# MoE 2, rounds 1 to 5: the seven products of a round in the order X, Y, X, Z, X, Z, X

## The chip, the cores and the metric

The kernel runs on one core of one Trainium2 chip. The metric is the device time of one execution in microseconds. Engines: PE is TensorE (matmuls; PEld its weight loads), DVE is VectorE, ACT is ScalarE, POOL is GpSimd, SP issues most of the DMAs.

## The reference

Attention with a local mask (heads 0 to 3) or a strided one (heads 4 to 7) on 4 x 8 heads of 576 x 64; its output, as 2304 tokens x 512, goes through two feed-forward blocks:

```
h = x @ w_in                      # MoE 1: 512 -> 2048
g = h * tanh(softplus(h))         # mish
x = g @ w_out                     # 2048 -> 512
g = x @ w_gate; silu = g * sigmoid(g)   # MoE 2: 512 -> 1536
val = x @ w_val
out = (silu * val) @ w_out        # 1536 -> 512
```

All in float32. Each fp32 operand is held as two parts (a high part rounded to fp32r, and the remainder), and each product of two operands is three matmuls: high x high, high x low, low x high (`mm3`, L160).

## The kernel before

The change is in MoE 2, in `c_round`. MoE 2 goes over 12 rounds: P = r // 6 picks a pair of token chunks of 512 (0 and 1, then 2 and 3), i = r % 6 picks 256 of the 1536 hidden columns. In a round, four outputs are wanted for gate (`g`) and for val (`v`): two chunks times two halves of 128 hidden columns. They are not made by eight products of blocks but by seven, with sums of weights (S12, S34) and sums of tokens (T1 to T4), in Winograd's manner. The table PROD names them, in the order n = 0 to 6: bank, weights, half, tokens.

Each product adds into one of three PSUM banks, X, Y or Z, with one such bank for gate and one for val: n = 0, 2, 4, 6 add into X, n = 1, 3 into Z, n = 5 is alone in Y. After every product the bank's state is read: after n = 0, 1, 2 ACT copies it to SBUF (L1327), after n = 3, 4, 5 DVE adds it to one of those copies (L1332), after n = 6 ACT takes silu of gate's bank (L1342) and DVE multiplies by val's (L1278). A product that adds into a bank on must therefore wait until the bank's earlier state has been read. A product is 6 matmuls (2 x mm3) for gate and 6 for val.

Rounds 0 and 6 to 11 take the products in the order n = 0 to 6 (X Z X Z X Y X). Rounds 1 to 5 take 0, 5, 1, 2, 3, 4, 6, that is X Y Z X Z X X. After the products of round r come 4 tiles `o` of the output product of the round before (`d_tile`, L1393: DVE adds each to `acc`), in rounds 0 to 5 the small last chunk (`c4_round`, tiles `c`), and 4 to 6 more tiles `o`.

In rounds 0 to 4 the other engines also make the weights of the round to come out of raw 64-bit data: units of 4 DVE instructions (L393, L396, L401, L404) and a Square on ACT (L398), or 2 DVE instructions for a sum (L370/L376 for S12, L372/L378 for S34); then ACT casts the high part (L150) and DVE subtracts it (L155) for the low part, in the middle of the next unit. The order of gate's units, then val's, is W0, W1, S12, S34, so the last of val's weights of a round are made in that round's first products.

The order on each engine is set when the program is built. The code is written in the order of PE's work, and `fill` puts background units between, by a model of time: `clk[...]` per engine, `on_dve`/`on_act` with costs in us, `pe_at` that holds PE's clock for an operand, `free`/`lru` for the banks, `gates` from which a unit may begin. `pe_at` changes no wait of the program; waits come from the data. SP and POOL run their queues in the order of the code.

Of the kernel before, what the change touches and what calls it, by code (L numbers as in the profile page):

```python
# [12 lines left out]
ALU = mybir.AluOpType  # L13
# [42 lines left out]
NP = FF2 // 256  # L56
LATE_OUT = ((), (1,), (3,), (5,), (7,), (8, 9))
SPLIT, SPLIT2, SUM2, SQUARE, MISH, COPY, LEAD = 0.69, 0.42, 0.42, 0.67, 0.6, 0.6, 0.2
# [47 lines left out]
def local_strided_attention__mish_moe__swiglu_kernel(  # L106
# [9 lines left out]
    nc = tc.nc  # L116
# [21 lines left out]
    def pe_at(t, what=None):  # L138
        clk["pe"] = max(clk["pe"], t)
# [75 lines left out]
    plan = []  # L215
# [28 lines left out]
    for r in range(NP):  # L244
        plan.append(("gate", ("n", r, -1)))
        todo = w2_out(*LATE_OUT[r])
        for kind in "gv"[r == 0:] if r + 1 < NP else "":
            todo += w2_in(kind, r + 1, "W0", "W1", "S12", "S34")
        for key in todo:
            if key[0][2] in ("S12", "S34"):  # L250
                plan.append(("gate", ("n", r, 2 if key[0][2] == "S12" else 4)))
            wlist.append(key)
            plan.append(("unit",))
    for n, k in enumerate(("T1", "T2", "B22", "T3", "B21", "T4")):
# [482 lines left out]
    def on_dve(cost, ready, do):  # L737
        clk["dve"] = max(clk["dve"], ready) + cost
        do()
        return clk["dve"]  # L740

    def on_act(cost, ready, do):
        clk["act"] = max(clk["act"], ready) + cost
        do()
        return clk["act"]
# [305 lines left out]

    def in_round(q, P, behind_=None):
        c0, c1 = 2 * P, 2 * P + 1
        bank, keep = [{}, {}], [{}, {}]
        for n, (x, a, half, b) in enumerate(PROD):
            if b[0] == "T":
                need(("x", P, b))
            for k in range(2):
                key = ("s", q, k, a)
                need(key if key[3][0] == "S" else ("i", q * QF + 2 * k + (a == "W1")))  # L1060
                first = x not in bank[k]
                if first:
                    bank[k][x] = lru("c" + x)
                p, at = bank[k][x]
                w = wt[key]
                for j in range(2):
                    sl = slice(half * 256 + j * 128, half * 256 + j * 128 + 128)
                    xo = x_op(P, b, j)
                    mm3(p, w[:, 0, sl], w[:, 1, sl], *xo, first and j == 0, j == 1, True)
                pe = clk["pe"]  # L1070
                if n < 3:
                    tag, nb = ("u", 4) if n < 2 else ("wtmp", 2)
                    keep[k][n] = t = sb.tile([128, 512], F32, tag=tag, name="k%d" % n, bufs=nb)
                    on_act(COPY, pe, lambda: nc.scalar.copy(t, p))
                    fill()
                elif n < 6:
                    fill()
                    t = keep[k][{3: 2, 4: 1, 5: 0}[n]]
                    r = on_dve(0.69, pe, lambda: nc.vector.tensor_tensor(out=t, in0=p, in1=t, op=ALU.add))
                    if n != 4:  # L1080
                        free(at, r)
                    r = mish(t, t, r)
                    g_make(q * NCH + (c0 if n == 5 else c1), [2 * k + (n == 4)], t, r)
                else:
                    if k == 0:
                        n6["t"] = sb.tile([128, 2, 512], F32, tag="acc4", name="n6")
                    n6[k] = n6["t"][:, k], mish(n6["t"][:, k], p, pe)
                    free(at, n6[k][1])
                    fill()
            if behind_:  # L1090
                behind_(n)
        gates["in", q, P] = clk["pe"]
# [166 lines left out]
    def ld(r, *what, kinds="gv"):  # L1259
        if r >= 2 * NP:  # L1260
            return
        P, i = divmod(r, NP)
        for x in what:
            for kind in "p" if x in (0, 1) else kinds:
                t = w2_slot(kind, r, x)
                if P == 0 and (2 * i + x in sum(LATE_OUT, ()) if kind == "p" else i > (kind == "g")):
                    continue
                half = x == "W1" and P == 1
                sl = slice(256 * half, 512)
                nc.sync.dma_start(t[:, :, sl].bitcast(F32), wd[kind, i, x][:, :, sl])  # L1270
                whole[kind, i, x] = moved("sp", clk["pe"], 0.5 if half else 1)
# [15 lines left out]
    def finish(r, f, c):  # L1287
# [9 lines left out]
        else:  # L1297
            for f in range(2):
                fs[r, f, c] = h[:, :, f * 256:f * 256 + 256], ready

    def c_round(r, between):
        P, i = divmod(r, NP)
        bank = {k: {} for k in "gv"}
        keep = {k: {} for k in "gv"}
        for n in (0, 5, 1, 2, 3, 4, 6) if 0 < r < NP else range(7):
            x, a, half, b = PROD[n]
            while (P, b) not in op_at:
                assert head()
                run_head()
            o = ops[P][b]  # L1310
            for k in "gv":
                need((k, i, a))
                first = x not in bank[k]
                if first:
                    bank[k][x] = lru("c" + x + k)
                p, at = bank[k][x]
                pe_at(op_at[P, b], (P, b))
                w = w2_slot(k, r, a)
                for j in range(2):
                    sl = slice(half * 256 + j * 128, half * 256 + j * 128 + 128)  # L1320
                    mm3(p, w[:, 0, sl], w[:, 1, sl], o[:, j, 0], o[:, j, 1], first and j == 0, j == 1, True)
                pe = clk["pe"]
                if n < 3:
                    tag, nb = ("u", 4) if n < 2 else ("wtmp", 2)
                    t = sb.tile([128, 512], F32, tag=tag, name="k%d" % n, bufs=nb)
                    keep[k][n] = t
                    on_act(COPY, pe, lambda: nc.scalar.copy(t, p))  # L1327
                    fill()
                elif n < 6:
                    fill()  # L1330
                    t = keep[k][{3: 2, 4: 1, 5: 0}[n]]
                    ready = on_dve(SPLIT, pe, lambda: nc.vector.tensor_tensor(out=t, in0=p, in1=t, op=ALU.add))  # L1332
                    if n != 4:
                        free(at, ready)
                    if k == "g":
                        s, silu = t, on_act(MISH, ready, lambda: nc.scalar.activation(out=t, in_=t, func=AF.Silu))  # L1336
                    else:
                        f, c = {3: (0, 1), 4: (1, 1), 5: (0, 0)}[n]
                        product(r, f, c, s, t, max(silu, ready))
                elif k == "g":  # L1340
                    s = sb.tile([128, 512], F32, tag="px", name="s21", bufs=2)
                    silu = on_act(MISH, pe, lambda: nc.scalar.activation(out=s, in_=p, func=AF.Silu))  # L1342
                    free(at, silu)
                    fill()
                else:
                    fill()
                    product(r, 1, 0, s, p, max(silu, pe), at)
            gates["n", r, n] = clk["pe"]
            between(n)
            fill()  # L1350

    def c4_round(r):
# [66 lines left out]
    with tc.manual_schedule():  # L1419
# [81 lines left out]
        for r in range(2 * NP + 1):  # L1501
            P = r // NP
            if r < 2 * NP:
                gates["n", r, -1] = clk["pe"]
                if r:
                    ld(r + 1, "W0")

                def between(n):
                    if r == 0:
                        if n == 5:  # L1510
                            settle("tiles")
                            ld(0, 0, 1)
                            ld(1, "W0", "S12", "S34")
                        return
                    if n == 2:
                        ld(r + 1, "S12")
                    if n == 4:
                        ld(r + 1, "S34")

                c_round(r, between)  # L1520
            if r > 0:
                for t in range(4):
                    d_tile(r - 1, 1, t)
            if r < 2 * NP:
                finish(r, 0, 0)
                finish(r, 1, 0)
                if P == 0:
                    c4_round(r)
                ld(r + 1, "W1")
            if r > 0:  # L1530
                for t in range(4):
                    d_tile(r - 1, 0, t)
                if r <= NP:
                    for t in range(2):
                        d_tile(r - 1, 4, t)
            if 0 < r < 2 * NP - 1:
                ld(r, 0, 1)
            if r == 2 * NP - 2:
                ld(r + 1, 0, 1)
# [86 lines left out]
```

## Time and profile before

| | |
|---|---|
| median of 3 runs | 865.35 us (865.15 to 868.08) |
| profiled execution | 864.76 us, span 863.0 us |
| PE busy | 851.2 us, 99% of the span |
| DVE busy | 624.3 us, 72% |
| ACT busy | 446.2 us, 52% |
| POOL busy | 175.1 us, 20% |
| MoE 2, rounds 1 to 5 | 467.16 to 665.82 us |

The profiled execution's own time is 1.76 us over its span. In the timeline a row is a group of like instructions; the duration of a group of matmuls reaches to the modelled end of its last, so that it overlaps the next by about 0.16 us. From start to start six matmuls of 128x512 take 1.36 us.

### The profile page before, as it was taken

The numbers are of one execution on the slowest core, as the hardware profiler recorded it, in microseconds if no ns is written. First come the engines' busy times: TensorE is split into PE (matmuls) and PEld (weight loads), VectorE is DVE, ScalarE is ACT, GpSimd is POOL, SyncE is SP. The second block draws the span as 40 slices with busy tenths as digits, with TensorE's granted clock in tenths as the row PEclk, the third lists the DMA queues.
The fourth block names the chain that finished last, engine by engine and source line by source line (L and its number), as shares of the span: only waits on it lengthen the run. The fifth ranks groups of instructions, "written<-read, shape, count | busy, mean of one in ns | idle before, by whom it ended". The sixth has DMA issues, their size and how long they took to land.

```text
span 863.0 us, 14267 instructions
## 1 busy us (share of the span) xinstructions
PE 851.2 (99%) x5216; PEld 707.2 (82%) x5216; DVE 624.3 (72%) x1348; ACT 446.2 (52%) x1063; POOL 175.1 (20%) x195
## 2 busy tenths in 40 slices
PE   8999999999999999999999999999999999999998
PEld 5788778888888888888888888887878888888886
DVE  6998879597668658685779999999987434432534
ACT  7999956565756565644645544444354322332230
POOL 5652311002010010002113202030216112211211
PEclk9999999999999999999999999999999999999999
DMA  9875344617867594753547655646491574464322
GB/s 300 267 222 165 114 162 189 223 51 150 276 153 226 139 267 109 220 216 123 226 164 231 221 211 191 225 170 239 147 320 60 181 270 139 153 209 136 108 84 98
DMA packets 46006, 158.72 MB, mean 184 GB/s; under 512 B 4976, under 2 KB 8688, under 8 KB 43632
## 3 DMA queue, kind: packets, MB, share of 16 engines
q1 hardware_dynamic: 40320, 129.81, 43.9%
q0 software_dynamic: 4464, 20.45, 9.5%
q10 hardware_dynamic: 1152, 7.55, 2.6%
q8 instruction: 41, 0.67, 0.3%
q14 instruction: 29, 0.24, 0.1%
HBM read 101.17 MB, written 56.62 MB: 183 GB/s over the span
## 4 chain that ended last, share of the span: by engine, by line
PE 91%; DVE 6%; issue 2%; ACT 1%; POOL 0%; DVEq 0%; POOLq 0%
PE y L160 23%; PE o L160 17%; PE h L160 8%; PE cX L160 8%; PE cXv L160 6%; PE cXg L160 6%; PE cZ L160 4%; PE c L160 3%; PE cZv L160 3%; PE cZg L160 3%; PE cY L160 2%; PE cYv L160 2%; PE cYg L160 2%; PE xp L599 2%; PE tp L562 2%
## 5 line engine op out<-in xcount | busy, mean ns | idle before, releaser
L160 PE MATMUL y<-g,w 128*128 128x512 f32 (+1 forms) x960 | 202.3, 370 | 0.0
L160 PEld LDWEIGHTS y<-g,w 128*128 128x128 f32 x960 | 166.7, 189 | 29.6
L160 PE MATMUL o<-wr,fs 128*128 128x512 f32 x648 | 149.6, 390 | 0.0
L160 PEld LDWEIGHTS o<-wr,fs 128*128 128x128 f32 x648 | 121.4, 188 | 25.0
L155 POOL TENSOR_TENSOR fs<-k,fs 128x512 fp32r<-128x512 f32 x36 | 50.2, 1393 | 269.3 <-ACT fs L150 251.5
L1393 DVE TENSOR_TENSOR acc<-acc,o 128x512 f32<-128x512 f32 x90 | 61.5, 684 | 35.5 <-PE o L160 35.2
L150 ACT CAST fs<-k 128x512 fp32r<-128x512 f32 x36 | 22.4, 622 | 80.6 <-DVE k L1278 35.5
L160 PE MATMUL h<-xh,w 128*128 128x512 f32 (+1 forms) x208 | 61.5, 361 | 0.0
L516 ACT ACTIVATE pt<-pt,sm 128x64 f32<-128x64 f32 (+1 forms) x160 | 55.9, 363 | 3.7 <-DVE sm L502 3.7
L160 PE MATMUL cXg<-T,wr 128*128 128x512 f32 x216 | 55.5, 393 | 2.2 <-DVE k L1332 2.0
L160 PE MATMUL cXv<-T,wr 128*128 128x512 f32 x216 | 55.2, 391 | 1.9 <-DVE k L1332 1.9
L1141 POOL DMA_DIRECT2D yd<-yv x20 | 16.0, 802 | 187.4 <-ACT yv L1135 187.4
L1327 ACT COPY k<-cXg 128x512 f32<-128x512 f32 x24 | 14.1, 587 | 75.8 <-PE cXg L160 75.8
L160 PEld LDWEIGHTS cXg<-T,wr 128*128 128x128 f32 x216 | 40.2, 188 | 12.4 <-DVE k L1332 4.3
L160 PEld LDWEIGHTS cXv<-T,wr 128*128 128x128 f32 x216 | 40.3, 188 | 11.5 <-DVE k L1332 3.2
L1332 DVE TENSOR_TENSOR k<-cZg,k 128x512 f32<-128x512 f32 x12 | 8.3, 688 | 49.5 <-PE cZg L160 49.5
L160 PEld LDWEIGHTS h<-xh,w 128*128 128x128 f32 x208 | 37.0, 189 | 5.2 <-issue 0.2
L1135 ACT COPY yv<-y 128x512 f32<-128x512 f32 x40 | 23.2, 588 | 28.7 <-PE y L160 26.2
L545 POOL TENSOR_TENSOR pt<-pt,sm 128x192 f32<-128x192 f32 (+2 forms) x48 | 34.1, 729 | 16.2 <-DVE sm L538 12.7
L160 PE MATMUL h<-xl,w 128*128 128x512 f32 (+1 forms) x104 | 36.4, 350 | 0.0
L1336 ACT ACTIVATE k<-k 128x512 f32<-128x512 f32 x36 | 22.8, 632 | 25.5 <-DVE k L1332 25.4
L160 PE MATMUL c<-yh,wr 128*128 128x256 f32 x192 | 35.5, 283 | 0.0
(180 smaller groups left out, 1807.8 us busy)
## 6 DMA issues: line engine op xcount, KB each, us to landing
raw<-in_w_dram SPq DMA_DIRECT2D x44, 512.0 KB, 4.9
rawl<-in_w_dram SPq DMA_DIRECT2D x24, 512.0 KB, 4.3
yd<-yv POOLq DMA_DIRECT2D x20, 512.0 KB, 5.9
wr<-wd_p SPq DMA_DIRECT2D x18, 512.0 KB, 4.4
wr<-wd_g_S SPq DMA_DIRECT2D x16, 512.0 KB, 3.4
wr<-wd_v_S SPq DMA_DIRECT2D x14, 512.0 KB, 4.6
wr<-wd_g_W SPq DMA_DIRECT2D x10, 512.0 KB, 6.3
wd_v_W<-wr SPq DMA_DIRECT2D x10, 512.0 KB, 5.0
```

The source lines that it names most:

```text
L150: nc.scalar.copy(hi, src)
L155: eng.tensor_tensor(out=lo, in0=src, in1=hi.bitcast(F32), op=ALU.subtract)
L160: nc.tensor.matmul(o, lhsT=lhs, rhs=rhs, start=first and i == 0, stop=last and i == 2, skip_group_check=more)
L516: nc.scalar.activation(out=pt[:, x], in_=pt[:, x], func=AF.Exp, scale=-1.0, bias=sm[:, 0, x:x + 1], accum_out=sm[:, 1, x:x + 1],)
L545: nc.gpsimd.tensor_tensor(out=a, in0=a, in1=sm[:, 1, x].unsqueeze(2).to_broadcast(a.shape), op=ALU.mult)
L562: nc.tensor.transpose(tp[:, 128 * x:128 * x + 128], a, ident)
L599: nc.tensor.matmul(banks[r][64 * h:64 * h + 64, o:o + nq - skip], lhsT=v_t[s][rows, i, 64 * h:64 * h + 64], rhs=ts[rows, c0 + skip:c0 + nq ...
L1135: t = on_act(COPY if nt == 512 else 0.4, clk["pe"], lambda: nc.scalar.copy(dst, p[:, :nt]))
L1141: nc.gpsimd.dma_start(yd[c][:, e0:e + 1], src, **kw)
L1327: on_act(COPY, pe, lambda: nc.scalar.copy(t, p))
L1336: s, silu = t, on_act(MISH, ready, lambda: nc.scalar.activation(out=t, in_=t, func=AF.Silu))
L1393: ready = on_dve(SPLIT, clk["pe"], lambda: nc.vector.tensor_tensor(out=x, in0=x, in1=o, op=ALU.add))
```

## The change

The order of the products in rounds 1 to 5 becomes 0, 5, 2, 1, 4, 3, 6 (X Y X Z X Z X): n = 2 is moved ahead of n = 1, and n = 4 ahead of n = 3. `LAST` says after which product the weights S12 and S34 are used for the last time, so that their gates and reloads stay at the same places (after the fourth and the sixth product). And `read` keeps the modelled time at which a bank was read, in `in_round` (MoE 1) and in `c_round`, and `pe_at` holds the next product on that bank to it.

```diff
@@ in_round (MoE 1)
-        bank, keep = [{}, {}], [{}, {}]
+        bank, keep, read = [{}, {}], [{}, {}], {}
...
+                pe_at(read.get((k, x), 0.0), (n, x))
...
-                    on_act(COPY, pe, lambda: nc.scalar.copy(t, p))
+                    read[k, x] = on_act(COPY, pe, lambda: nc.scalar.copy(t, p))
...
-                    r = on_dve(0.69, pe, lambda: nc.vector.tensor_tensor(out=t, in0=p, in1=t, op=ALU.add))
+                    read[k, x] = r = on_dve(0.69, pe, lambda: nc.vector.tensor_tensor(out=t, in0=p, in1=t, op=ALU.add))
@@ c_round (MoE 2)
+    ROUND = range(7), (0, 5, 2, 1, 4, 3, 6)
+    LAST = {False: {2: "S12", 4: "S34"}, True: {1: "S12", 3: "S34"}}
...
-        for n in (0, 5, 1, 2, 3, 4, 6) if 0 < r < NP else range(7):
+        read = {}
+        for n in ROUND[0 < r < NP]:
...
-                pe_at(op_at[P, b], (P, b))
+                pe_at(max(op_at[P, b], read.get((k, x), 0.0)), (P, b, k))
...
-                    on_act(COPY, pe, lambda: nc.scalar.copy(t, p))
+                    read[k, x] = on_act(COPY, pe, lambda: nc.scalar.copy(t, p))
...
-                    ready = on_dve(SPLIT, pe, lambda: nc.vector.tensor_tensor(out=t, in0=p, in1=t, op=ALU.add))
+                    read[k, x] = ready = on_dve(SPLIT, pe, lambda: nc.vector.tensor_tensor(out=t, in0=p, in1=t, op=ALU.add))
...
             gates["n", r, n] = clk["pe"]
-            between(n)
+            done = LAST[0 < r < NP].get(n, n)
+            gates["n", r, done] = clk["pe"]
+            between(done)
@@ the gates of the units and the reloads on SP
-                plan.append(("gate", ("n", r, 2 if key[0][2] == "S12" else 4)))
+                plan.append(("gate", ("n", r, key[0][2])))
...
-                    if n == 2:
-                        ld(r + 1, "S12")
-                    if n == 4:
-                        ld(r + 1, "S34")
+                    if n in ("S12", "S34"):
+                        ld(r + 1, n)
```

What this moves on PE, in each of the rounds 1 to 5 (round 1 here; `cXg` is gate's bank X, `cZv` val's bank Z; T and B are the token operands; `+` is the order after the change):

```order
 L160 MATMUL cYg<-B_5126,wr 128x512 x6
 L160 MATMUL cYv<-B_5126,wr 128x512 x6
+L160 MATMUL cXg<-T_5046,wr 128x512 x6
+L160 MATMUL cXv<-T_5046,wr 128x512 x6
 L160 MATMUL cZg<-T_4800,wr 128x512 x6
 L160 MATMUL cZv<-T_4800,wr 128x512 x6
-L160 MATMUL cXg<-T_5046,wr 128x512 x6
-L160 MATMUL cXv<-T_5046,wr 128x512 x6
+L160 MATMUL cXg<-T_5022,wr 128x512 x6
+L160 MATMUL cXv<-T_5022,wr 128x512 x6
 L160 MATMUL cZg<-B_5109,wr 128x512 x6
 L160 MATMUL cZv<-B_5109,wr 128x512 x6
```

The pair on T_5046 (n = 2) stands ahead of the pair on T_4800 (n = 1), and the pair on T_5022 (n = 4) ahead of that on B_5109 (n = 3); the last pair on X (n = 6) follows in both orders. The rest of PE's order is the same.

On DVE, the stretch of round 2 that reads the fifth and the sixth product (k are the SBUF copies, rawl and wt a unit of weights). Before:

```order
L155 TENSOR_TENSOR wr<-wt_5804,wr 128x512
L1332 TENSOR_TENSOR k_5846<-cZg,k_5846 128x512
L1332 TENSOR_TENSOR k_5860<-cZv,k_5860 128x512
L1278 TENSOR_TENSOR k_5846<-k_5846,k_5860 128x512
L393 TENSOR_SCALAR wt_5877<-rawl 128x512
L1332 TENSOR_TENSOR k_5826<-cXg,k_5826 128x512
L396 SCALAR_TENSOR_TENSOR wt_5877<-rawl,wt_5877 128x512
L1332 TENSOR_TENSOR k_5835<-cXv,k_5835 128x512
L1278 TENSOR_TENSOR k_5826<-k_5826,k_5835 128x512
```

And after the change:

```order
L155 TENSOR_TENSOR wr<-wt_5804,wr 128x512
L1337 TENSOR_TENSOR k_5845<-cXg,k_5845 128x512
L1337 TENSOR_TENSOR k_5860<-cXv,k_5860 128x512
L1279 TENSOR_TENSOR k_5845<-k_5845,k_5860 128x512
L393 TENSOR_SCALAR wt_5877<-rawl 128x512
L1337 TENSOR_TENSOR k_5825<-cZg,k_5825 128x512
L396 SCALAR_TENSOR_TENSOR wt_5877<-rawl,wt_5877 128x512
L1337 TENSOR_TENSOR k_5833<-cZv,k_5833 128x512
L1279 TENSOR_TENSOR k_5825<-k_5825,k_5833 128x512
```

The reads of X and of Z have changed places; no background instruction stands elsewhere between them. On ACT the copies of X and of Z (the third and the fourth product) change places in the same way, in round 2 without any other row moving. The orders of SP and POOL are the same, and so is everything in MoE 1.

## Rows read from the trace of the kernel before

**Rows 1.** The page, busy time of each engine over the span.

```profile
PE 851.2 (99%) x5216; PEld 707.2 (82%) x5216; DVE 624.3 (72%) x1348; ACT 446.2 (52%) x1063; POOL 175.1 (20%) x195
```

**Rows 2.** Waits of PE, whole span: line, releaser, us in total, times, longest.

```profile
PE cXg L160 <- DVE k L1332: 2.0, 2, 1.4
PE cXv L160 <- DVE k L1332: 1.9, 3, 0.6
```

**Rows 3.** Timeline of PE, round 2: start, duration, instructions, [idle before, releaser].

```profile
506.52 1.52 PE L160 MATMUL cXg<-B,wr 128*128 128x512 f32 x6
...
521.48 1.52 PE L160 MATMUL cXv<-T,wr 128*128 128x512 f32 x6
523.06 1.65 PE L160 MATMUL cXg<-T,wr 128*128 128x512 f32 x6
525.35 1.66 PE L160 MATMUL cXv<-T,wr 128*128 128x512 f32 x6 [0.64 <-DVE k L1332]
526.84 5.60 PE L160 MATMUL o<-wr,fs 128*128 128x512 f32 x24
```

**Rows 4.** Timeline of DVE and POOL around the end of round 2's products.

```profile
519.99 0.68 DVE L1332 TENSOR_TENSOR k<-cZg,k 128x512 f32<-128x512 f32 x1
520.59 0.68 DVE L1332 TENSOR_TENSOR k<-cZv,k 128x512 f32<-128x512 f32 x1
...
522.32 0.68 DVE L1332 TENSOR_TENSOR k<-cXg,k 128x512 f32<-128x512 f32 x1
522.86 1.29 POOL L155 TENSOR_TENSOR fs<-k,fs 128x512 fp32r<-128x512 f32 x1 [20.23 <-ACT fs L150]
522.92 1.77 DVE L396 SCALAR_TENSOR_TENSOR wt<-rawl,wt 128x512 int32<-128x512 int32 x1
...
524.62 0.68 DVE L1332 TENSOR_TENSOR k<-cXv,k 128x512 f32<-128x512 f32 x1
...
528.40 0.69 DVE L1393 TENSOR_TENSOR acc<-acc,o 128x512 f32<-128x512 f32 x1 [0.32 <-PE o L160]
```

**Rows 5.** Timeline of PE, rounds 1, 3, 4, 5: n = 4 val, and first o.

```profile
482.22 1.52 PE L160 MATMUL cXv<-T,wr 128*128 128x512 f32 x6
...
487.14 5.60 PE L160 MATMUL o<-wr,fs 128*128 128x512 f32 x24
...
561.18 1.52 PE L160 MATMUL cXv<-T,wr 128*128 128x512 f32 x6
...
566.59 5.61 PE L160 MATMUL o<-wr,fs 128*128 128x512 f32 x24
...
600.94 1.52 PE L160 MATMUL cXv<-T,wr 128*128 128x512 f32 x6
...
606.29 5.60 PE L160 MATMUL o<-wr,fs 128*128 128x512 f32 x24
...
640.63 1.52 PE L160 MATMUL cXv<-T,wr 128*128 128x512 f32 x6
...
646.44 5.60 PE L160 MATMUL o<-wr,fs 128*128 128x512 f32 x24
```

**Rows 6.** Round 2 whole: stretch, us, busy by engine, granted clock, DMA share, GB/s.

```profile
506.52:546.22 39.70, 39.00 (x193) 32.64 (x192) 37.27 (x60) 17.10 (x30) 7.10 (x5) 1.00 0.57 199
```

**Rows 7.** Timeline of DVE, PEld and ACT at the starts of rounds 2 and 3.

```profile
507.32 0.68 DVE L155 TENSOR_TENSOR wr<-wt,wr 128x512 fp32r<-128x512 f32 x1
507.65 1.32 PEld L160 LDWEIGHTS cXv<-B,wr 128*128 128x128 f32 x6
...
509.44 0.59 ACT L1327 COPY k<-cXv 128x512 f32<-128x512 f32 x1 [0.25 <-PE cXv L160]
...
545.82 0.68 DVE L155 TENSOR_TENSOR wr<-wt,wr 128x512 fp32r<-128x512 f32 x1
...
547.36 1.32 PEld L160 LDWEIGHTS cXv<-B,wr 128*128 128x128 f32 x6
...
548.92 0.69 DVE L155 TENSOR_TENSOR wr<-wt,wr 128x512 fp32r<-128x512 f32 x1 [1.01 <-ACT wr L150]
```

## The prediction

> **What bounds the kernel now.** First the page's list of busy times: PE is busy 99% of the span, the next engine, DVE, 72% [rows 1]. So a gain can only come out of PE's gaps, and the next question is where they are. The table of waits, for PE over the whole span, has one pair of rows on the lines of this change: the two X banks wait for the DVE addition that reads them, 3.9 us in five waits [rows 2]. That is less than what they cost, since a matmul that waited also starts its pipeline anew and the one at 523.06 bears no mark. So I read the loss from start times instead, in the timeline of PE. In round 2 the eleven pieces from 506.52 (n = 0, gate) to 521.48 (n = 4, val) take 14.96 us, 1.36 us each; from 521.48 to the first o there are three pieces (n = 4 val, n = 6 gate, n = 6 val), 4.08 us by that measure, but o starts at 526.84, after 5.36 us: 1.28 us are lost [rows 3].
>
> The timeline of DVE beside it shows why. n = 4 and n = 6 are neighbours on X. The addition that reads gate's X starts at 522.32 and ends at 523.00, and n = 6 gate starts at 523.06 where its place was 522.84. Then DVE's next instruction, L396, takes 1.77 us, beside a POOL instruction that started at 522.86; the addition that reads val's X comes behind it, 524.62 to 525.30, and n = 6 val starts at 525.35, 0.93 us behind a gate piece that ended its 1.36 us at 524.42 [rows 3, 4]. 0.22 + 0.93 is 1.15 us; the other 0.13 us goes into the last piece, 1.49 us from its start to o instead of 1.36.
>
> **The change part by part.** It adds no instruction and takes none away; five rounds have their products, their reads and their copies exchanged.
>
> *The last wait on X.* In the new order n = 4 is the fifth product and n = 3 stands between it and n = 6. Its reads take the places that the reads of Z had: in round 2 at 519.99 and 520.59, ending at 520.67 and 521.27 [rows 4]. n = 6 would start at 522.84 for gate and 524.20 for val, so that 2.1 and 2.9 us are to spare. Nothing in DVE's order ahead of these reads has changed, and nothing that they wait for: the fifth product ends where it did. So the whole loss of a round should go. By the same subtraction as above (first o less n = 4 val less 4.08): round 1 0.84, round 2 1.28, round 3 1.33, round 4 1.27, round 5 1.73 us [rows 3, 5]. Sum: 6.45 us. Bounds: nothing goes (0), if the wait is another's, and 6.45, for PE has no more to give in these places.
>
> *What is late next on the banks.* The reads of Z now come last, one of them behind the slow L396, at 524.62. No product follows on Z; the next user of a bank that is freed then is the tile o or c, and c begins four o behind the products (24 matmuls, 5.4 us at the measure above). I cost this at nothing. X's third product (n = 2) now has one product between it and n = 0 instead of two. It needs ACT's copies of n = 0: val's is done at 510.03, 3.51 us into the round, and n = 2 val starts at 5 x 1.36 = 6.80 us [rows 7, 3]. 3.3 us to spare; cost nothing. S12 and S34 are first used by the third and the fifth product in either order, so no weight is wanted earlier.
>
> *DVE and the weights of the next round.* This is the cover that becomes thin. DVE is busy 37.27 of the 39.70 us of round 2 [rows 6]; PE without its 1.28 us would need 38.42. At the end of a round DVE makes the low part of val's W0 for the next. I take L155 at 507.32 and at 545.82 for it, by the order of the units. The first weight load that needs it is the third of `cXv` in the next round's first product: 507.65 + 2 x 0.227 = 508.10, against 508.00 when L155 ends: 0.1 us to spare at the start of round 2. At the start of round 3 it is 547.81 against 546.50: 1.31 us [rows 7]. If PE comes earlier by 0.84 and 1.28 us and DVE does not, PE waits here 0.74 us at round 2 and nothing at round 3. But DVE does come earlier, since it waits for PE itself: 0.32 us at the first o of round 2 [rows 4]. With that row as the measure, round 2 would start with a wait of 0.84 - 0.32 - 0.10 = 0.42 us, and rounds 3 to 5 with none (0.35 us to spare). It doesn't add up from round to round: early in each round DVE waits 1.01 us for a cast that stands behind ACT's copy of the first product, so that it starts from PE's time again, with a little less of that second [rows 7]. I take 0.4 us, bounds 0 and 0.74.
>
> At this place a rule of the Trainium skill bears on the case. The row first: POOL's subtraction at 522.86 and L396, 1.77 us against the 0.68 of the DVE rows around it, ending 0.54 us behind POOL, while additions that read PSUM kept 0.68 [rows 4]. The skill (SBUF — State Buffer, Who interferes with whom) says that a DVE instruction with two SBUF inputs and a POOL instruction that reads SBUF exclude each other, whichever starts second waits for the end of the first, and an instruction with one SBUF input does not contend. The row agrees. By the rule PE's earlier arrival, which lets POOL start its later subtractions earlier, can turn a collision on or off on DVE; that is part of the second rival below.
>
> *The model of emission.* `pe_at` with the reads changes the builder's clock only. The built orders show that it moved no row outside the exchanged ones, so its cost is nothing.
>
> *Sum.* 6.45 - 0.4 = 6.05 us. Against the profiled execution's own 864.76 us that gives 858.7; the median, 865.35, is 0.59 us above it and would give 859.3. I forecast 859.0 us.
>
> **The rivals.**
>
> *DVE is the next bound.* For: 37.27 of 39.70 us busy, and 0.1 us of slack at round 2 [rows 6, 7]. If DVE kept its times, rounds 1 to 4 would together gain only what slack there is, 0.1 + 1.31 us, and round 5, which makes no more weights, its 1.73: 3.1 us, 861.6 us. If on top a POOL instruction (1.29 us) fell anew on DVE's path in each of four rounds, with 0.35 us to spare, 4 x 0.94 = 3.8 us would go from 6.05: 2.3 us gained, 862.5. Against: the 1.01 and 0.32 us that DVE waits for PE, which are slack that comes along [rows 4, 7].
>
> *The wait is not the bank's, so nothing changes.* What else n = 6 could wait for is W1. Its low part for val is made early in the round (548.92 in round 3), some 16 us before n = 6 val; and n = 6 starts 0.06 and 0.05 us after the additions end [rows 3, 4, 7]. 864.8 us.
>
> *Slower: the copies of n = 0 become the wait.* ACT's copy of X must now be done one product earlier. Price: each us by which it passes 6.80 us into the round stops PE for it, in five rounds. With 3.3 us to spare it would have to come 4.6 us later than now to cost more than the 1.3 us that a round gains; at 5.6 us late the kernel would be about 5 us slower, 870 us. For: the copies stand in one queue with casts that wait for DVE. Against: the copy came 0.25 us after its product, and ACT is busy 17.10 of 39.70 us [rows 6, 7].
>
> The granted clock is 1.00 in round 2, with its gaps [rows 6]; I see nothing in closing them that would change it.
>
> **How the numbers follow.** The forecast's case 0.75: with 0 to 0.74 us for the weights, and the two bases, 858.3 to 859.7, and some tenths for what a run differs. DVE as the next bound 0.15: 861.6 to 862.5. Nothing changes 0.06: 864.8. Slower 0.04: 870. The range from 857.6 to 862.1 leaves out the two last cases and about half of the second, less than 0.2. A measurement of this kernel can tell a change from none at about 0.5%, 4.3 us: below 861.0 faster, above 869.7 slower. So faster has the first case and a little of the second, 0.77; the same has the rest of it and the third, 0.19; slower 0.04.
>
> **What would show it.** In the profile after: the table of waits has no row of X for L1332's successor; from n = 3 val to the first o there are 4.1 us in each of the five rounds; round 2 to round 3 takes 38.4 to 38.5 us instead of 39.70. The weights' term is right if PE or its weight loads wait for L155 at `cXv` of round 2 by some tenths, and at no other round. The prediction is wrong if waits of that kind stand at the starts of rounds 3 to 5, or if n = 2 waits for ACT's copy, or if the time is above 861.

## The result and the profile after

The kernel after takes 858.13 us (median of 6 runs, 857.83 to 859.09), the kernel before, beside it, 866.10 us (6 runs, 865.15 to 868.08): a ratio of 0.991, interval 0.9896 to 0.9921. The forecast was 859.0 us. The profiled execution took 858.39 us against 864.76, its span 856.2 us against 863.0.

The page of the kernel after, the row of busy times and the chain of work that ended last, by engine, and the same chain in the kernel before:

```profile
PE 848.8 (99%) x5216; PEld 707.6 (83%) x5216; DVE 623.2 (73%) x1348; ACT 446.2 (52%) x1063; POOL 177.0 (21%) x195
```

```profile
PE 97%; ACT 1%; DVE 1%; POOL 0%; issue 0%; POOLq 0%
```

```profile
PE 91%; DVE 6%; issue 2%; ACT 1%; POOL 0%; DVEq 0%; POOLq 0%
```

The engines do the same work as before [rows 1]. PE's 2.4 us less of busy time are the part of its loss that was counted as busy; its idle time fell by 4.4 us (from 11.8 to 7.4), and both together are the 6.8 us by which the span is shorter. In the chain, DVE's 6% are down to 1%. PE's table of waits has no row of an X bank any more; those of before were [rows 2].

The timeline of PE, round 2, answering to [rows 3]; start, duration, instructions:

```profile
505.60 1.52 PE L160 MATMUL cXg<-B,wr 128*128 128x512 f32 x6
...
517.84 1.52 PE L160 MATMUL cXv<-T,wr 128*128 128x512 f32 x6
519.20 1.52 PE L160 MATMUL cZg<-B,wr 128*128 128x512 f32 x6
520.56 1.52 PE L160 MATMUL cZv<-B,wr 128*128 128x512 f32 x6
521.92 1.52 PE L160 MATMUL cXg<-T,wr 128*128 128x512 f32 x6
523.28 1.52 PE L160 MATMUL cXv<-T,wr 128*128 128x512 f32 x6
524.64 5.60 PE L160 MATMUL o<-wr,fs 128*128 128x512 f32 x24
```

From 505.60 to 524.64 stand fourteen pieces at 1.36 us each, with nothing between them. From n = 3 val (520.56) to the first o are 4.08 us; in rounds 1, 3, 4 and 5 it is 4.08 us too (482.14 to 486.22 and so on).

DVE and POOL at the same place, answering to [rows 4] (the reads are at L1337 now):

```profile
519.14 0.68 DVE L1337 TENSOR_TENSOR k<-cXg,k 128x512 f32<-128x512 f32 x1
519.74 0.68 DVE L1337 TENSOR_TENSOR k<-cXv,k 128x512 f32<-128x512 f32 x1
...
521.47 0.69 DVE L1337 TENSOR_TENSOR k<-cZg,k 128x512 f32<-128x512 f32 x1
522.07 1.79 DVE L396 SCALAR_TENSOR_TENSOR wt<-rawl,wt 128x512 int32<-128x512 int32 x1
523.78 0.68 DVE L1337 TENSOR_TENSOR k<-cZv,k 128x512 f32<-128x512 f32 x1
```

```profile
522.00 1.30 POOL L155 TENSOR_TENSOR fs<-k,fs 128x512 fp32r<-128x512 f32 x1 [20.29 <-ACT fs L150]
```

The reads of X end at 519.82 and 520.42 and their products start at 521.92 and 523.28: 2.1 and 2.9 us to spare, as forecast. In rounds 1 and 5, where an L155 stands between the two reads, the least is 2.0 us (481.54 to 483.50, round 1). The long L396 beside POOL's subtraction is still there, 1.79 us. It now delays the read of Z, for which no product waits.

The window of round 2, columns as in [rows 6]:

```profile
505.60:544.02 38.42, 38.42 (x194) 32.79 (x192) 36.35 (x59) 17.11 (x30) 7.65 (x5) 1.00 0.59 206
```

Round 2 takes 38.42 us instead of 39.70, the figure that the prediction had for PE without its loss, and PE is busy in all of it; rounds 3 to 5 take 38.42 us too, round 1 38.53. From the start of round 1 to the start of the last tiles o, behind round 11, which is 467.16 to 837.18 before and 467.07 to 830.64 now, 370.02 us have become 363.57: 6.45 us less. Of the 6.8 us by which the span is shorter, 0.09 came before round 1 and 0.26 at the end. Outside its span the profiled execution took 2.19 us, 0.43 more than before's 1.76, so that 6.37 us are left between the two executions' own times.

### The profile page after: what moved, and what is told of

It is laid out like the page before. It is cut to its first block, busy times and chain, and to the rows that moved or that the text cites. A ratio compares the mean times of both kernels' runs of the same rounds, so it can differ in the third digit from the quotient of the medians.

```text
span 856.2 us, 14263 instructions
## 1 busy us (share of the span) xinstructions
PE 848.8 (99%) x5216; PEld 707.6 (83%) x5216; DVE 623.2 (73%) x1348; ACT 446.2 (52%) x1063; POOL 177.0 (21%) x195
## 4 chain that ended last, share of the span: by engine, by line
PE 97%; ACT 1%; DVE 1%; POOL 0%; issue 0%; POOLq 0%
PE y L160 23%; PE o L160 17%; PE h L160 8%; PE cX L160 8%; PE cXv L160 8%; PE cXg L160 8%; PE c L160 4%; PE cZ L160 4%; PE cZv L160 4%; PE cZg L160 4%; PE cYg L160 2%; PE cYv L160 2%; PE cY L160 2%; PE xp L599 2%; PE tp L562 2%; PE sc L482 1%
## 5 line engine op out<-in xcount | busy, mean ns | idle before, releaser
L155 POOL TENSOR_TENSOR fs<-k,fs 128x512 fp32r<-128x512 f32 x36 | 51.8, 1438 | 263.2 <-ACT fs L150 246.7
L1337 DVE TENSOR_TENSOR k<-cZg,k 128x512 f32<-128x512 f32 x12 | 8.2, 687 | 49.5 <-PE cZg L160 49.5
```

The source lines that it names most:

```text
L155: eng.tensor_tensor(out=lo, in0=src, in1=hi.bitcast(F32), op=ALU.subtract)
```

## Experiments

**The kernel before, once more.** No edit. How much do its time and its stalls differ from run to run?

> The kernel before once more, with a second profile. If the five stalls at n = 6 are the whole difference of MoE 2, they should sum to 6.45 us again within 0.3 us, and the rounds 1 to 5 take 198.7 us. If instead the stalls vary from run to run (the median of before is 1.3 us above its profiled run, that of after 0.3 us below its own), this profile, when its time is near 866, shows the sum of the stalls 1 us or more above 6.45.

865.11 us, ratio 0.9996 (0.9982 to 1.0010). By the subtraction of the prediction its profiled execution (866.68 us) lost 0.83, 1.30, 1.30, 1.28 and 1.73 us in the five rounds: 6.44. So the loss has the same sum, to 0.01 us, in both profiled executions, and rounds 1 to 5 took 198.65 us, as expected; the rival that the stalls vary is out. What varied was another place: round 1 starts at 469.10 instead of 467.16. The window of the first 60 us, which holds attention and the first products `h` of MoE 1, has a granted clock of 0.97, where the first profile has 1.00:

```profile
0.00:60.00 60.00, 57.02 (x878) 41.13 (x879) 49.05 (x294) 52.93 (x260) 32.44 (x59) 0.97 0.83 259
```

In the same 60 us PE issued 878 matmuls instead of 888. The lower clock lies between 16 and 24 us (0.90 and then 0.68 in two windows of 4 us, where the first profile has 1.00 in both); why it fell in this execution stays open. In the other comparisons the median of before was 865.67 (19 runs) and 864.75 (22 runs): 6.6 to 7.5 us above 858.13, where the first comparison has 8.0.

**Neighbours on X, but where ACT reads.** The order X Y Z X X Z X: n = 2 and n = 4 are neighbours on X, and the state between them is read by ACT's copy, not by DVE. Without the model's holds in `pe_at` (those lines are not shown), and with `LAST` fitted to the order.

```diff
-    ROUND = range(7), (0, 5, 2, 1, 4, 3, 6)
-    LAST = {False: {2: "S12", 4: "S34"}, True: {1: "S12", 3: "S34"}}
+    ROUND = range(7), (0, 5, 1, 2, 4, 3, 6)
+    LAST = {False: {2: "S12", 4: "S34"}, True: {2: "S12", 3: "S34"}}
```

> Rounds 1 to 5 in the order X Y Z X X Z X: n = 4 still ahead of n = 3, but n = 2 and n = 4 are now neighbours on X, and what is read between them is read by ACT's copy. My theory: neighbours on a bank cost only what the reading engine is late; ACT copies within 0.8 us of a piece's end, a piece takes 1.36 us, so nothing is lost: within 0.1% of the changed kernel, no wait of X in the profile. Rival: two products in a row on one bank cost by themselves about the 1.3 us a round that the kernel before lost: 864.6 us. A small loss (0.1 to 0.3 us a round) would say that ACT's copy is only just in time.

859.23 us (4 runs, 858.16 to 860.34), ratio 0.9923 (0.9903 to 0.9942). That median is 0.13% above the 858.13 of another comparison, a little over the expected 0.1%; but the profiled execution took 858.16 us against 858.39, and the rounds take 38.53 and then 38.42 us, the same as in the kernel after. No wait on X. The timelines of PE and of ACT in round 2:

```profile
514.93 1.52 PE L160 MATMUL cXv<-T,wr 128*128 128x512 f32 x6
516.29 1.52 PE L160 MATMUL cXg<-T,wr 128*128 128x512 f32 x6
517.65 1.52 PE L160 MATMUL cXv<-T,wr 128*128 128x512 f32 x6
```

```profile
516.49 0.59 ACT L1331 COPY k<-cXv 128x512 f32<-128x512 f32 x1 [0.77 <-PE cXv L160]
```

Val's copy starts at 516.49, when n = 2 val ends (514.93 + 1.52 = 516.45), and is done at 517.08; n = 4 val starts on the same bank at 517.65, in its place. A pair on a bank has 1.36 us for the read, since gate's and val's pieces alternate. ACT needs 0.59 and comes at once. So neighbours as such cost no time where the reader between them is in time.

**The model alone.** The old order with all the rest of the change (`read`, `pe_at`).

```diff
-    ROUND = range(7), (0, 5, 2, 1, 4, 3, 6)
-    LAST = {False: {2: "S12", 4: "S34"}, True: {1: "S12", 3: "S34"}}
+    ROUND = range(7), (0, 5, 1, 2, 3, 4, 6)
+    LAST = {False: {2: "S12", 4: "S34"}, True: {2: "S12", 4: "S34"}}
```

> The second part of the change alone: the products in the order of before (X Y Z X Z X X), the model of emission with the reads. With the order of after, the model moves no row; with this order it puts DVE's reads of the tiles o some rows later. My theory: n = 6 still waits for the same additions, so the time is that of before within 0.3%, stalls of about 6.4 us in rounds 1 to 5. Rival: the model does the work by moving background out of the reads' way: more than 0.4% faster than before.

866.00 us, ratio 1.0001 (0.9991 to 1.0011), and 0.81, 1.28, 1.29, 1.31 and 1.75 us lost in the rounds, 6.44 in all. The waits on X stand as in [rows 2], of which val's here is:

```profile
PE cXv L160 <- DVE k L1337: 1.9, 3, 0.6
```

In the old order the model takes no time out. In the new one it moves no row: the new order built without the holds is the same program, instruction by instruction on every engine. The whole gain is the order's.

**The old order, its two reads earlier.** If DVE is late because it takes weight instructions ahead of the additions, then the old order must do without the loss if these come behind. For n = 4 of rounds 1 to 5 `fill` is left out.

```diff
-                    fill()
+                    if n != 4 or not 0 < r < NP:
+                        fill()
```

> The order of before (X Y Z X Z X X), but in rounds 1 to 5 no background is put ahead of DVE's two additions that read n = 4, so that in rounds 2 to 4 L393 and L396 stand behind them. My theory: the stall is what stands ahead of the reads in DVE's queue, not the neighbourhood of n = 4 and n = 6: in rounds 2 to 4 the reads end 0.2 us or more before n = 6 wants the bank, and 3.9 of the 6.45 us go; rounds 1 and 5 keep most of theirs (0.8 and 1.7 us), since DVE is late there for other reasons: about 0.45% faster than before. Rival (neighbours cost by themselves, by the latency from the end of a product through the addition to the next): the time of before within 0.1%.

860.59 us, ratio 0.9939 (0.9922 to 0.9956). Round 2 on PE, and DVE with POOL beside it:

```profile
521.30 1.52 PE L160 MATMUL cXv<-T,wr 128*128 128x512 f32 x6
522.67 1.55 PE L160 MATMUL cXg<-T,wr 128*128 128x512 f32 x6
524.06 1.53 PE L160 MATMUL cXv<-T,wr 128*128 128x512 f32 x6
525.42 4.92 PE L160 MATMUL o<-wr,fs 128*128 128x512 f32 x21
```

```profile
522.94 0.69 DVE L1333 TENSOR_TENSOR k<-cXv,k 128x512 f32<-128x512 f32 x1 [0.44 <-PE cXv L160]
...
524.90 0.69 DVE L396 SCALAR_TENSOR_TENSOR wt<-rawl,wt 128x512 int32<-128x512 int32 x1
525.63 1.68 DVE L401 SCALAR_TENSOR_TENSOR wt<-rawl,wt 128x512 int32<-128x512 int32 x1
```

```profile
525.32 1.45 POOL L155 TENSOR_TENSOR fs<-k,fs 128x512 fp32r<-128x512 f32 x1 [1.33 <-issue]
```

4.12 us from 521.30 to o, so 0.04 lost where it was 1.28; in rounds 3 and 4 it is 0.04 and 0.03. DVE now waits for PE ahead of val's read instead of the other way round. Rounds 1 and 5 keep 0.84 and 1.78, so that 3.7 us of the 6.45 went, where 3.9 were expected. In these two rounds it is gate's read that is late, behind an L155 between the reads of Z and the L1278 of n = 3, which this edit doesn't move. Of round 5, in the kernel before:

```profile
641.10 1.29 POOL L155 TENSOR_TENSOR B<-ys,B 128x512 fp32r<-128x512 f32 x1 [20.24 <-DVE k L1332]
641.15 1.78 DVE L1278 TENSOR_TENSOR k<-k,k 128x512 f32<-128x512 f32 x1
642.86 0.68 DVE L1332 TENSOR_TENSOR k<-cXg,k 128x512 f32<-128x512 f32 x1
```

Gate's read ends at 643.54, and n = 6 gate starts at 643.59. Here it is L1278 that takes 1.78 us beside POOL. That the 0.84 and 1.73 us of rounds 1 and 5 come from this is read from such rows; no run moved these instructions alone. The second finding is in the last rows of round 2 above: L396, away from POOL, takes 0.69 us, and L401, now beside POOL's next subtraction, takes 1.68.

**Val's read alone.** How the loss divides between gate's read, late by the short L393, and val's, late by L396 beside POOL.

```diff
-                    fill()
+                    if (n, k) != (4, "v") or not 0 < r < NP:
+                        fill()
```

> The order of before; in rounds 1 to 5 background may stand ahead of DVE's read of gate's n = 4 (L393), but none ahead of the read of val's (L396 goes behind it). It splits the loss of rounds 2 to 4 between the two. My theory: of 1.28 to 1.33 us a round, 0.2 to 0.3 us belong to gate's read, late by L393, and about 1.05 us to val's, late by L396 beside POOL: the stalls of rounds 2 to 4 fall to about 0.25 us each, 3.1 us less than before in all, rounds 1 and 5 unchanged. Rival: L393 ahead of gate's read shifts both, and val's read then runs into the next POOL instruction: half of the loss or more (0.6 us a round) stays.

862.01 us, ratio 0.9964 (0.9953 to 0.9974). What is left in rounds 2 to 4 is 0.36, 0.35 and 0.40 us, from rows such as these of round 2:

```profile
522.82 1.52 PE L160 MATMUL cXv<-T,wr 128*128 128x512 f32 x6
524.41 1.65 PE L160 MATMUL cXg<-T,wr 128*128 128x512 f32 x6
525.90 1.52 PE L160 MATMUL cXv<-T,wr 128*128 128x512 f32 x6
527.26 1.07 PE L160 MATMUL o<-wr,fs 128*128 128x512 f32 x4
```

In all 2.75 us went, where 3.1 were expected. Gate's read costs 0.37 us a round (0.23 before the piece starts and 0.13 in it, 1.49 us long), val's 1.29 - 0.37 = 0.92. I had read 0.22 and 0.93 and left 0.13 in the last piece: it belongs to whichever piece waited.

**More work on DVE, to find the next bound.** The kernel after, and in rounds 1 to 4, behind the products, additional instructions on DVE of 128x480 whose result changes nothing.

```diff
+                if 0 < r < NP - 1:
+                    for _ in range(2):
+                        nc.vector.tensor_tensor(out=cst, in0=cst, in1=cst, op=ALU.max)
```

> The changed kernel with two more DVE instructions (an elementwise maximum of the constants with themselves, 128x480, about 0.57 us each) behind the products of each of the rounds 1 to 4; nothing uses them. It measures how near the weights of the next round (val's W0, low part) are to being the bound. My theory (slack as read in the changed kernel's trace: 0.10 us at round 2, 0.78 to 0.81 us at rounds 3 to 5; DVE can take back 0.3 us in round 1, where it waits for PE's tiles, and nothing in rounds 2 to 4): waits at val's first product of round 2 of about 0.75 us and of rounds 3 to 5 of about 0.35 us each, 1.8 us in all, 860.0 us. Rival (DVE has room elsewhere, in the waits for ACT early in a round): no wait and no change against the changed kernel. Rival 2 (DVE is the bound already): 4 x 1.14 = 4.6 us.

863.03 us, ratio to the kernel before 0.9979 (0.9969 to 0.9990): 4.9 us more than the kernel after in its comparison (863.38 against 858.39, 5.0 us, between the profiled executions), where 1.8 were expected. The place is the expected one. PE's waits, and round 3's start:

```profile
PE cXv L160 <- DVE wr L155: 3.0, 4, 0.8
```

```profile
545.56 1.52 PE L160 MATMUL cXg<-B,wr 128*128 128x512 f32 x6
546.92 0.61 PE L160 MATMUL cXv<-B,wr 128*128 128x512 f32 x2
548.34 1.20 PE L160 MATMUL cXv<-B,wr 128*128 128x512 f32 x4 [0.80 <-DVE wr L155]
549.37 0.85 PE L160 MATMUL cYg<-B,wr 128*128 128x512 f32 x3
```

From n = 0 val to the next piece are 2.45 us instead of 1.36: 1.09 us lost, and by the same rows 0.88, 1.10 and 1.09 at the other three, 4.2 us in all. The size was missed because the two instructions did not take the 1.14 us that were expected of them:

```profile
566.84 2.32 DVE L1528 TENSOR_TENSOR cst<-cst 128x480 f32<-128x480 f32 x2
```

```profile
567.11 1.53 POOL L155 TENSOR_TENSOR fs<-k,fs 128x512 fp32r<-128x512 f32 x1 [2.73 <-issue]
```

Alone one takes 0.65 us; the second ran into POOL's next subtraction. In the kernel after, at this place, POOL's 1.77 us begin during a DVE row that is already running, and then meet a row that reads PSUM and takes 0.68 us:

```profile
564.46 1.77 POOL L155 TENSOR_TENSOR fs<-k,fs 128x512 fp32r<-128x512 f32 x1 [2.74 <-issue]
```

```profile
564.38 0.69 DVE L404 SCALAR_TENSOR_TENSOR wt<-wr,wt 128x512 f32<-128x512 f32 x1
564.99 0.68 DVE L1279 TENSOR_TENSOR s<-s,cXv 128x512 f32<-128x512 f32 x1
```

**Four instead of two.** The same with `range(4)`.

> The same with four more instructions a round, 2.28 us. My theory: past the slack each us costs a us: waits of about 1.9 us at round 2 and 1.5 us at rounds 3 to 5, 6.4 us in all, 864.5 us, all at val's first product of a round. Rival (room elsewhere): under 3 us in all. Rival 2 (DVE the bound already): 9.1 us.

870.30 us, ratio to the kernel before 1.0061 (1.0042 to 1.0081); 6.4 us were expected over the kernel after, and it is 12.2.

```profile
PE cXv L160 <- DVE wr L155: 8.5, 4, 2.2
```

At the starts of rounds 2 to 5 PE loses 2.28, 2.46, 2.46 and 2.44 us, 9.6 in all; the profiled execution (867.61 us) lies 9.2 us above that of the kernel after. Two more instructions cost 1.37 us a round more, and they take 1.39 us more on DVE (3.71 us for the four, 2.32 for the two): from here on each microsecond on DVE is one on PE. The median is another 2.7 us above this execution, which is the shortest of seven (867.61 to 872.68). Five of the others, 868.80 to 872.68, have a mean granted clock of 0.996 to 0.998, where this one and the run of 869.01 have 1.00; at which place the clock fell, no profile of them shows.

## Why the prediction was right

**The loss at n = 6.** 6.45 us were forecast, and the stretch of the rounds is 6.45 us shorter. That the wait was the bank's, and the lateness DVE's order with POOL behind it, is shown by the two early-read kernels: with the reads first and the old order, the loss of rounds 2 to 4 goes too, all but 0.04 us a round. The rival that the wait is another's falls with it. The loss of rounds 1 and 5, 2.57 of the 6.45 us, stays in those kernels and goes with the new order; what makes DVE late there is read from rows and not tested by a run.

**Banks that are read late now.** Nothing was charged for the reads of Z and for the copies of n = 0, and nothing came. ACT's copy of n = 0 val, before which ACT waited 0.26 us for the product, begins 2.92 us into the round:

```profile
508.52 0.59 ACT L1332 COPY k<-cXv 128x512 f32<-128x512 f32 x1 [0.26 <-PE cXv L160]
```

It is done at 509.11, and n = 2 val starts at 512.40: 3.3 us to spare, as forecast. So the slower rival has no ground.

**The weights of the next round: the term that was mis-sized.** It took 0.4 us for a wait at the start of round 2; there is none. Of DVE and PEld, round 2, answering to [rows 7], and of DVE at round 3:

```profile
505.05 0.68 DVE L404 SCALAR_TENSOR_TENSOR wt<-wr,wt 128x512 f32<-128x512 f32 x1
505.80 0.69 DVE L1397 COPY acc<-o 128x512 f32<-128x512 f32 x1
506.41 0.68 DVE L155 TENSOR_TENSOR wr<-wt,wr 128x512 fp32r<-128x512 f32 x1
...
544.14 0.68 DVE L155 TENSOR_TENSOR wr<-wt,wr 128x512 fp32r<-128x512 f32 x1
```

```profile
506.74 1.32 PEld L160 LDWEIGHTS cXv<-B,wr 128*128 128x128 f32 x6
...
545.15 0.87 PEld L160 LDWEIGHTS cXv<-B,wr 128*128 128x128 f32 x4
```

L155 ends at 507.09, the third load stands at 506.74 + 2 x 0.227 = 507.19: 0.10 us to spare, as before. DVE came forward by 0.91 us (507.32 to 506.41) where PE came by 0.92. The step that failed was to give DVE only the 0.32 us that it waits for PE at the first o of round 2. For this term, the end of round 1 was the place to look at, and there DVE is paced by PE's last o: the copy at 505.80 begins 0.04 us after that tile's modelled end (505.60 + 0.16), although the instruction ahead of it began at 505.05 and the next could follow after 0.60. The same gap is in the kernel before, unmarked because it is short:

```profile
505.96 0.68 DVE L404 SCALAR_TENSOR_TENSOR wt<-wr,wt 128x512 f32<-128x512 f32 x1
506.72 0.69 DVE L1390 COPY acc<-o 128x512 f32<-128x512 f32 x1
507.32 0.68 DVE L155 TENSOR_TENSOR wr<-wt,wr 128x512 fp32r<-128x512 f32 x1
```

L155 stands right behind an instruction that waits for PE's own output, by 0.16 us before and 0.15 after, so it kept its distance to PE, and the term should have been nothing. At round 3 the slack is 545.15 + 0.45 - 544.82 = 0.78 us, where 0.35 was forecast and 1.31 was there before: in round 2 DVE came forward by another 0.77 us (1.68 in all, 545.82 to 544.14), not by 0.32. The 1.01 us that the prediction gives to DVE's early wait in each round is that of rounds 3 to 5; in round 2 it was 0.41, in the kernel before as after.

**DVE as the next bound.** It is the rival that comes nearest and isn't reached: two more instructions a round cost 4.2 us at just the wait that it names. With the DVE work as it is, 0.10 us remain at round 2 and 0.78 to 0.81 at rounds 3 to 5. What the prediction had against this rival, DVE's own waits for PE, decided.

**The model of emission** at nothing: shown with the old order by its time, with the new one by the built order.

**The sum.** 6.05 us were forecast for 6.45 in the rounds; 858.7 us from the profiled execution, which took 858.39. Without the 0.4 us the same sum gives 858.31; that this is within 0.1 us of the measured time is luck, since 0.35 us less outside the rounds and 0.43 us more outside the span nearly cancel. The 859.0 lay between the profiled execution's sum and the one on the median. The medians differ by more than the rounds do (8.0 us, and 6.6 to 7.5 against the other two medians of before); in the longer execution of the kernel before that was profiled, 1.94 us of the time came ahead of round 1.

POOL's lock on DVE, the place where the prediction drew on the Trainium skill (SBUF — State Buffer, Who interferes with whom), holds in the kernel after and in two experiments: L396 takes 1.79 us beside POOL and 0.69 away from it, L401 1.68 beside it, and one of two added instructions waited, while a multiplication that reads PSUM keeps 0.68 beside POOL (564.99 above). In [rows 4] themselves only one addition overlaps POOL's row there, and it had begun before. For an instruction with one SBUF input the prediction leaves out a condition that this section of the Trainium skill gives, that it is outside the 2-port perf modes. Here one such row, L393, takes 1.20 us at 538.83, beside POOL's 538.44 to 539.74, and 0.42 alone; whether it ran in such a mode, no row shows. The new order doesn't remove the collision. In rounds 2 to 5 it puts it behind the last read that a product needs.

## What to carry to other kernels

When a sequence adds on in a few banks, look for the pair of neighbours on one bank whose state between them is read by an engine that comes late, and put another bank's product there; here neighbours whose reader was in time cost nothing. Read what a wait costs from start times at the engine's full pace, since the table of waits had 3.9 us of 6.45. And before a wait is charged to an engine that comes closer, see what it did just before: if it had to wait there for the bound engine's output, the two move together.

## What was not expected of the hardware

A matmul group that had to wait for its bank loses more than the gap: from its start to the next it took 1.49 us instead of 1.36, val's in the kernel before [rows 3] and gate's in the one with val's read early. And DVE instructions of 128x480 that take 0.65 us alone took up to 1.64 us where they met POOL: a pair took 2.32 us.
